# A fused recurrence and feed-forward kernel on one core: another written-out order of the same steps

## Chip, core and metric

One core of a Trainium2 chip. The metric is the device time of one execution in microseconds; the kernel before took 248.06 us as the median of three runs (247.24 to 250.97).

## The reference

Inputs are r, k, v, w, a, b of shape (4, 8, 768, 40): batch, heads, time, head dimension. A state of 40 x 40 for each batch and head is carried over 768 time steps; its outputs are the rows of a feed-forward block with a squared ReLU.

```python
for t in range(S):
    y[:, :, t] = np.einsum('bhd,bhde->bhe', rt, state)
    Sa = np.einsum('bhde,bhe->bhd', state, at)
    state_decay = state * wt[:, :, None, :] - np.einsum('bhd,bhe->bhde', Sa, bt)
    state = state_decay + np.einsum('bhd,bhe->bhde', vt, kt)
...
x = attn_out.transpose(0, 2, 1, 3).reshape(B * S, H * D)      # 3072 x 320
h = x @ w_in                                                  # 320 x 2048
g = np.maximum(h, 0.0) ** 2
return g @ w_out                                              # 2048 x 320
```

## The kernel before

The 768 steps are cut into 12 chunks (c = 0 to 11) of 64 steps. Within a chunk the recurrence is done with matmuls: products of decays are cumulative sums of log w, a unit-triangular system is solved by one correction, and the state goes from chunk to chunk. The 256 output rows of a chunk (4 batches x 64 steps) then go through the feed-forward block.

The kernel is a list of named steps. A step is an instruction on VectorE, ScalarE or GpSimd, a set of matmuls on PE, or one or two DMA issues; the number behind its name is the chunk. Steps that the text speaks of:

- Loads on SP: `ldw`, `ldk`, `ldb`, `lda`, `ldv`, `ldr` bring one tensor of one chunk into `raw_w`, `raw_kb`, `raw_a`, `raw_v`, `raw_r` (two buffers each; k and b share one), two issues of 160 KB. `lwi 0 k. x.` brings a quarter of one half of w_in's first 256 rows into a `G` buffer, `lwl 0` the last 64 rows into the buffer `CX` of odd chunks, `lwo 0 x.` an eighth of w_out into an `osb` buffer. `st` stores an output.
- Casts to bf16: `castK`, `castB`, `castA`, `castR`, `castV`; `cwi` makes `WIN`, `cwl` makes `WLAST`, `cwo` makes `WOUT`. For chunks 3 and later k and b are not cast but multiplied (`mulKB`).
- Decays: `ln` (logarithm of w), `hi` and `lo` (its two bf16 parts), `ci` and `cf` (cumulative sums on PE), `ex`, `ei`, `exw`, `ef`, `eg` (their exponentials).
- Turns on PE with identities: `TA`, `TR`, `TK`, `BK`, `TV`, `TS`, `XT`; their results leave PSUM by `tA`, `tR` or `tRw`, `tK`, `bK`, `tV`, `tS`, `xt`.
- Solve and state: `EN` (masked by `mEN`), `AS`, `EV`, `NU` (with `u0` and `u1` behind them), `SC`, `S` (with `s`, the new state `STb`). Output: `CX` (masked by `mCX`), `RS`, `Y` (with `y`, `yd`).
- Feed-forward: `F` and `FL` (eight matmuls on `WIN`, four on `WLAST`, for each quarter u0 to u3), `f` (ReLU), `q` (square), `O` (matmuls on `WOUT`), `o`.

A step's dependences come from what it reads and writes, buffers included. All PSUM results share four buffers, and an entry of the order such as `PE2` names the buffer that the step takes. Some steps can run on several engines, and the order names the engine. So three things are set by hand, by the text `ORDER`: the sequence on each engine's queue, the engine, and the PSUM buffer. `Plan.issue` reads it from left to right and emits:

```python
for entry in text.replace("\n", " ").split(";"):
    where, name = entry.split(None, 1)
    ...
    eng = where.rstrip("0123456789")
    assert i not in done and done.issuperset(o.preds), name
    ...
    for h in o.alloc:
        self.slot_of[h] = int(where[len(eng):])
    if o.emit[0] == "pe":
        for f in o.emit[2]:
            f()
    else:
        o.emit[1][eng]()
```

Each engine does its queue in sequence, and an instruction that waits holds up what stands behind it. SP's queue holds all loads but half of the first; a load into a buffer in use waits for the step that empties it. Because helpers emit everything, L390 is the line of nearly all matmuls, L394 and L397 those of the turns, L371 and L373 those of VectorE copies, L376 of ScalarE copies, L380 of GpSimd casts.

Of the kernel before, what the change touches and what calls it, by code (L numbers as in the profile page):

```python
# [91 lines left out]
eg 1; DVE mEN 0 g0; ACT ef 1; SP ldb 2; DVE castB 1; PE2 EV 0; DVE bK 0; SP ldv 1; PE3 TK 1; ACT
u0 0; PE0 TA 1; DVE tK 1 g1; ACT ln 2; POOL castR 0; PE NU 0; PE1 TR 0; DVE tA 1 g0; ACT u1 0 g0;
POOL castK 2; DVE tK 1 g0; SP lda 2; ACT u1 0 g1; POOL hi 2; ACT tRw 0; PE2 S 0 g0; POOL lo 2; PE
S 0 g1; DVE tA 1 g1; SP lwi 0 k1 x1; PE3 TV 0; DVE s 0 q0; SP ldw 3; POOL castB 2; PE0 cf 2; DVE s
0 q1; ACT tV 0; PE1 EN 1 g0; POOL castV 1 g1; DVE mEN 1 g0; PE2 EN 1 g1; SP lwi 0 k1 x3; SP lwo 0
x0; POOL castA 2; ACT eg 2; PE3 AS 1; DVE mEN 1 g1; PE1 TK 2; SP ldr 1; ACT castV 1 g0; DVE tK 2
g0; PE2 BK 1; ACT ef 2; SP lwl 0; PE EV 1; DVE tK 2 g1; ACT bK 1; PE0 TS 0; SP lwi 0 k1 x0; DVE u0
1; SP lwi 0 k0 x3; PE2 CX 0 g1; ACT tS 0; PE1 TA 2; DVE mCX 0 g1; SP ldv 2; PE NU 1; PE0 ci 2; DVE
tA 2 g1; ACT u1 1 g0; DVE tA 2 g0; ACT u1 1 g1; PE2 EN 2 g1; POOL castR 1; SP lwi 0 k1 x2; DVE mEN  # L100
2 g1; ACT exw 2; PE1 SC 1; SP lwi 0 k0 x1; PE3 TR 1; ACT ln 3; SP lwi 0 k0 x0; PE S 1 g0; PE S 1
g1; ACT tRw 1; SP lwi 0 k0 x2; PE2 CX 0 g0; POOL cwl 0; DVE s 1 q1; PE0 TV 1; SP lda 3; ACT hi 3;
DVE s 1 q0; POOL cwo 0 x0; PE3 BK 2; ACT tV 1; DVE mCX 0 g0; POOL lo 3; PE1 EN 2 g0; SP ldk 3; DVE
# [6 lines left out]
q1; SP lda 4; ACT castR 2; DVE mCX 1 g0; PE0 F 0 u2; ACT f 0 u1; SP ldv 3; PE1 TA 3; DVE cwo 0 x1;  # L110
ACT q 0 u0; PE2 TR 2; DVE tA 3 g0; PE3 RS 1; DVE tA 3 g1; PE Y 1; ACT tRw 2; POOL mulKB 3 h0; PE
FL 0 u2; SP lwo 0 x2; DVE y 1; PE1 TV 2; ACT f 0 u2; DVE yd 1; DVE mulKB 3 h1; PE2 FL 0 u3; ACT tV
2; POOL q 0 u2; PE3 XT 1; PE0 TK 3; SP lwo 0 x3; DVE xt 1; SP ldw 4; PE F 0 u3; DVE tK 3; ACT q 0
u1; POOL castV 3 g0; PE1 CX 2 g1; PE3 FL 1 u1; ACT f 0 u3; DVE mCX 2 g1; PE0 EN 3 g0; POOL castV 3
g1; PE F 1 u1; ACT cwo 0 x2; DVE mEN 3 g0; SP ldr 3; PE2 F 1 u2; ACT f 1 u1; POOL cwo 0 x3; PE1 EN
# [6 lines left out]
ldw 5; PE0 SC 3; DVE tV 3; PE S 3 g0; ACT castA 4; PE S 3 g1; PE2 cf 4; DVE s 3 q1; PE1 XT 2; ACT
ef 4; PE O 0 u1; DVE mulKB 4 h0; ACT xt 2; SP ldr 4; DVE mulKB 4 h1; PE2 TR 3; ACT cwo 0 x6; PE O
0 u2; DVE s 3 q0; ACT tRw 3; SP ldv 4; DVE cwo 0 x7; PE1 TA 4; PE0 TK 4; DVE tA 4 g1; PE2 CX 3 g1;
ACT tK 4; PE O 0 u3; DVE tA 4 g0; SP lda 6; DVE mCX 3 g1; PE1 F 2 u0; ACT o 0; PE2 CX 3 g0; ACT ln
5; PE0 EN 4 g0; DVE mCX 3 g0; PE3 FL 2 u3; PE FL 2 u0; POOL hi 5; PE F 2 u3; SP ldw 6; ACT f 2 u0;
DVE mEN 4 g0; POOL lo 5; PE2 F 2 u2; ACT q 1 u2; PE1 EN 4 g1; SP ldb 5; ACT f 2 u3; POOL q 2 u0;
# [24 lines left out]
O 3 u1; ACT ef 7; SP ldk 8; ACT ex 7 h0 g0; PE NU 6; ACT castR 6; PE2 TA 7; DVE u1 6 g0; ACT q 4
u2; PE0 TK 7; SP ldv 8; PE O 3 u2; DVE u1 6 g1; ACT tK 7; DVE tA 7 g0; PE O 3 u3; DVE tA 7 g1; DVE
hi 8; PE3 TR 6; DVE o 3; PE2 SC 6; POOL lo 8; ACT tR 6 g0; PE S 6 g0; PE S 6 g1; ACT tR 6 g1; PE0
XT 5; SP lda 9; DVE s 6 q1; PE1 TV 6; ACT xt 5; POOL castV 7 g1; PE3 TS 5; DVE tV 6; PE0 F 5 u0;
ACT tS 5; SP ldr 7; DVE s 6 q0; PE FL 5 u0; POOL castV 8 g1; PE1 ci 8 h0; ACT f 5 u0; PE3 EN 7 g0;
SP lda 8; POOL castV 7 g0; PE2 FL 5 u1; DVE mEN 7 g0; PE F 5 u1; POOL q 4 u3; ACT ex 8 h0 g1; ACT
# [929 lines left out]
```

## Time and profile before

| | |
|---|---|
| median of three runs | 248.06 us (247.24, 248.06, 250.97) |
| the profiled execution's own time | 247.57 us |
| its span | 245.6 us |
| busy: PE, PE weight loads | 222.8 us (91%), 176.5 us (72%) |
| busy: VectorE, ScalarE, GpSimd | 187.3 (76%), 173.4 (71%), 121.8 us (50%) |
| mean granted TensorE clock | 0.975 |
| DMA | 33.54 MB in 102,248 packets, 89,014 of them under 512 B |

The span is what the trace covers; the profiled execution's own time is 1.97 us longer and is comparable with the runs. A busy share is an average over a start, in which loads land, and a long dense part, in which PE hardly stands still, so the stages have to be read apart. A matmul's listed duration overlaps with that of its neighbours; the distance from start to start says what it costs.

### The profile page before, as it was taken

Reading aid. Unit: us, or ns where it says so; the run is one execution under the profiler, and the core shown is the slowest. Engines: PE = TensorE matmul, PEld = TensorE weight load, DVE = VectorE, ACT = ScalarE, POOL = GpSimd, SP = SyncE. Lnnn points to the kernel's source line nnn. Section 1 sums busy time; section 2 is a strip of 40 time slices with the busy share of each in tenths; the row PEclk is TensorE's granted clock in tenths of the full one; section 3 lists DMA queues with packets and bytes.
Section 4 is the critical chain, followed back from the end, with each engine's and each line's share of the span. In section 5 each row is a group of like instructions: output and inputs, shape, how many; then the busy total and the mean of one; then the engine's idle time right before and its main releaser. Section 6 shows DMA issues by size and latency. Waiting matters only on the chain.

```text
span 245.6 us, 12235 instructions
## 1 busy us (share of the span) xinstructions
PE 222.8 (91%) x5584; PEld 176.5 (72%) x5584; DVE 187.3 (76%) x234; ACT 173.4 (71%) x223; POOL 121.8 (50%) x111
## 2 busy tenths in 40 slices
PE   0668848999999999999999999999999899999993
PEld 0457737778887878778777777776877678887872
DVE  8589964888859878879989778798799788876600
ACT  3496963789788997977989757876876455660931
POOL 8245307528490887561619695327467940330150
PEclk9979985999999999999999999999999999999998
DMA  6998999989899988996984477687364020000403
GB/s 156 222 183 190 195 252 167 200 199 225 199 173 175 179 186 151 181 170 161 154 197 105 112 175 155 106 165 138 84 131 91 3 56 5 3 5 0 109 0 106
DMA packets 102248, 33.54 MB, mean 137 GB/s; under 512 B 89014, under 2 KB 101814, under 8 KB 101942
## 3 DMA queue, kind: packets, MB, share of 16 engines
q1 hardware_dynamic: 101014, 32.45, 64.0%
q8 instruction: 43, 0.70, 1.2%
q10 hardware_dynamic: 1184, 0.33, 0.6%
q14 instruction: 7, 0.06, 0.1%
HBM read 28.84 MB, written 3.93 MB: 133 GB/s over the span
## 4 chain that ended last, share of the span: by engine, by line
PE 77%; DMA 6%; DVE 6%; SPq 5%; ACT 3%; issue 1%; POOL 1%; ACTq 0%; POOLq 0%; DVEq 0%
PE pb L390 65%; PE pb L394 7%; PE pb L397 5%; DMA raw_r<-in_r_dram 3%; DMA raw_w<-in_w_dram 2%; DVE EN L689 1%; SPq L413 1%; SPq L443 1%; DMA raw_kb<-in_k_dram 1%; SPq L421 1%; DVE G L934 1%; DVE KBT L512 1%; DVE G L930 1%; SPq L1011 1%; ACT VUT L376 1%
## 5 line engine op out<-in xcount | busy, mean ns | idle before, releaser
L936 POOL TENSOR_TENSOR G<-G 128x1024 bf16<-128x1024 bf16 x25 | 47.6, 1911 | 40.1 <-ACT G L928 20.2
L390 PE MATMUL pb<-WOUT,G 128*128 128x320 bf16 (+1 forms) x400 | 57.3, 294 | 0.5 <-DVE G L930 0.5
L928 ACT ACTIVATE G<-pb 128x1024 bf16<-128x1024 f32 x41 | 41.5, 1022 | 18.4 <-PE pb L390 17.9
L390 PE MATMUL pb<-XT,WIN 128*128 128x256 bf16 x384 | 47.8, 273 | 0.4 <-ACT Gin L574 0.4
L390 PEld LDWEIGHTS <-G 128*128 128x128 bf16 x400 | 36.4, 98 | 14.2 <-issue 1.5
L390 PEld LDWEIGHTS <-WIN 128*128 128x128 bf16 x384 | 35.0, 98 | 7.7 <-issue 2.9
L689 DVE TENSOR_TENSOR CX<-pb,MSKI 128x1024 bf16<-128x1024 f32 x24 | 29.2, 1218 | 4.7 <-PE pb L390 3.4
L689 DVE TENSOR_TENSOR EN<-pb,MSK 128x1024 bf16<-128x1024 f32 x24 | 29.0, 1219 | 4.6 <-PE pb L390 4.4
L384 POOL TENSOR_TENSOR KB<-raw_kb,iG 128x640 bf16<-128x640 f32 x12 | 18.7, 1569 | 18.3 <-ACT iG L568 13.2
L384 POOL TENSOR_TENSOR lo<-lnW,hi 128x640 bf16<-128x640 f32 x11 | 16.0, 1458 | 17.2 <-PE pb L394 6.6
L781 DVE TENSOR_TENSOR STb<-pb,GT 64x640 bf16<-64x640 f32 x22 | 18.1, 821 | 8.2 <-POOL WLAST L380 5.5
L658 DVE TENSOR_TENSOR AR<-pb,GT 128x512 bf16<-128x512 bf16 x24 | 15.8, 684 | 6.4 <-PE pb L394 3.5
L390 PE MATMUL pb<-XT,WLAST 64*128 64x256 bf16 x192 | 17.1, 271 | 0.0
L590 ACT ACTIVATE GT<-pb 128x1024 f32<-128x1024 f32 x12 | 12.3, 1022 | 6.6 <-PE pb L390 4.0
L574 ACT ACTIVATE Gin<-pb 64x320 f32<-64x320 f32 x36 | 15.0, 426 | 2.6 <-PE pb L390 2.2
L376 ACT ACTIVATE AR<-pb 128x512 bf16<-128x512 bf16 (+1 forms) x15 | 10.2, 710 | 9.1 <-PE pb L397 4.0
L859 DVE TENSOR_TENSOR Yb<-pb,Gin 128x640 bf16<-128x640 f32 (+1 forms) x24 | 12.4, 552 | 5.0 <-PE pb L390 4.9
L390 PEld LDWEIGHTS <-EN 64*64 64x64 bf16 x768 | 14.0, 109 | 2.8 <-issue 1.7
L390 PE MATMUL pb<-UTI,hi 64*128 64x64 bf16 x192 | 8.3, 199 | 6.8 <-ACT hi L376 6.8
L376 ACT ACTIVATE VU<-pb 64x640 bf16<-64x640 f32 x15 | 10.5, 698 | 4.9 <-PE pb L390 3.7
L568 ACT ACTIVATE iG<-pb 128x640 f32<-128x640 f32 x18 | 12.6, 698 | 1.3 <-PE pb L390 1.2
L938 ACT ACTIVATE G<-G 128x1024 bf16<-128x1024 bf16 x12 | 12.6, 1054 | 0.1
(113 smaller groups left out, 439.9 us busy)
## 6 DMA issues: line engine op xcount, KB each, us to landing
raw_kb<-in_b_dram SPq DMA_DIRECT2D x24, 160.0 KB, 4.2
raw_kb<-in_k_dram SPq DMA_DIRECT2D x24, 160.0 KB, 4.6
raw_a<-in_a_dram SPq DMA_DIRECT2D x24, 160.0 KB, 3.6
raw_v<-in_v_dram SPq DMA_DIRECT2D x24, 160.0 KB, 4.4
raw_w<-in_w_dram SPq DMA_DIRECT2D x23, 160.0 KB, 4.8
raw_r<-in_r_dram SPq DMA_DIRECT2D x22, 160.0 KB, 5.1
out_dram<-osb SPq DMA_DIRECT2D x22, 160.0 KB, 3.1
osb<-in_moe_w_out_dram SPq DMA_DIRECT2D x8, 320.0 KB, 4.9
```

The costliest lines, as they stand in the source:

```text
L376: alts.append(("ACT", c_act(n), lambda: nc.scalar.activation(out=o_(), in_=i_(), func=ACTF.Copy, scale=1.0 if scale is None else scale)))
L384: return [("POOL", 40 + 2.35 * n, lambda: nc.gpsimd.tensor_tensor(out=o_(), in0=a_(), in1=b_(), op=op)), ("DVE", c_dve(n), lambda: nc.vect ...
L390: return lambda: nc.tensor.matmul(out=o_(), lhsT=l_(), rhs=r_(), start=start, stop=stop, skip_group_check=True)
L394: return lambda: nc.tensor.transpose(out=o_(), in_=i_(), identity=IDb[rows(g), :])
L568: ew(f"ei {c} h{jh}", [("ACT", c_act(2 * n), lambda hb=hb, jh=jh: nc.scalar.activation(out=iG[0][:].rearrange("p (g j) e -> p g (j e)", g= ...
L574: nc.scalar.activation(out=Gin[c % NGI][rows(g), NP * jh:NP * jh + NP, :].rearrange("p j e -> p (j e)"), in_=slot(hb, FP32)[rows(g), g, 0: ...
L658: ew(f"tA {c} g{g}", [("DVE", c_dve(512), lambda g=g: nc.vector.tensor_tensor(out=steps(AR[q2][:, 0, g]), in0=turned(ha, g), in1=steps(GT[ ...
L689: evac(f"m{nm} {c} g{g}", lambda s, n: [("DVE", c_dve(n), lambda: nc.vector.tensor_tensor(out=dst[q2][:, g, s].rearrange("p q i t -> p (q ...
L781: ew(f"s {c} q{q}", [("DVE", c_dve(2 * n), lambda q=q: nc.vector.tensor_tensor(out=STb[q2][rows(q), :, q, 0:D], in0=slot(hs, FP32)[rows(q) ...
L928: ("ACT", c_act(1024), lambda gb=gb, hf=hf: nc.scalar.activation(out=gb, in_=slot(hf, FP32)[:], func=ACTF.Relu)),
L936: ("POOL", 1900, lambda gv=gv: nc.gpsimd.tensor_tensor(out=gv, in0=gv, in1=gv, op=ALU.mult)),
L938: ("ACT", c_act(1024), lambda gv=gv: nc.scalar.activation(out=gv, in_=gv, func=ACTF.Square))],
```

## The change

Only the text `ORDER` changes. The steps, buffers and matmuls are the same, and each engine gets its steps in another sequence; some steps go to another engine and many PSUM results to another of the four buffers. The new sequence was laid out by a planner that was given longer transfers and scattered landing times. Changes of the matmul array's shape between neighbouring steps on PE number 201 before and 198 now. VectorE has 207 steps where it had 214, ScalarE 232 where it had 224 (two DMA issues among them), GpSimd 93 where it had 94.

```diff
-ORDER = """SP ldw 0; SP ldb 0; SP ldk 0; SP lda 0; ACT ln 0; SP ldw 1; ACT hi 0; DVE castB 0; DVE lo 0; DVE
-castK 0; PE0 cf 0; SP ldk 1; POOL castA 0; PE1 ci 0; ACT ef 0; SP lda 1; PE2 TA 0; SP ldv 0; ACT
...
+ORDER = """SP ldw 0; SP ldk 0; SP ldb 0; SP ldw 1; ACT ln 0; DVE hi 0; DVE lo 0; SP lda 0; PE0 cf 0; POOL
+castB 0; SP ldk 1; POOL castK 0; ACT eg 0; PE1 TK 0; SP ldb 1; ACT ln 1; PE2 ci 0; DVE tK 0 g0;
...
```

SP's queue at the loads of chunk 2, before:

```order
11 L453 DMA raw_r_84<-in_r_dram 128x1x320 x2
12 L421 DMA raw_kb_80<-in_k_dram 128x1x320 x2
13 L421 DMA raw_kb_80<-in_b_dram 128x1x320 x2
14 L436 DMA raw_v_87<-in_v_dram 64x16x40 x2
15 L443 DMA raw_a_82<-in_a_dram 128x1x320 x2
16 L1011 DMA G_128<-in_moe_w_in_dram 32x2048
```

and now:

```order
11 L453 DMA raw_r_84<-in_r_dram 128x1x320 x2
12 L421 DMA raw_kb_80<-in_b_dram 128x1x320 x2
13 L443 DMA raw_a_82<-in_a_dram 128x1x320 x2
14 L436 DMA raw_v_87<-in_v_dram 64x16x40 x2
15 L1011 DMA G_128<-in_moe_w_in_dram 32x2048
16 L421 DMA raw_kb_80<-in_k_dram 128x1x320 x2
```

k of chunk 2 (`ldk 2`) moved from the first of these five loads to the last, behind b, a, chunk 1's v and a quarter of half of w_in.

SP's queue at the loads of w_in, before:

```order
20 L453 DMA raw_r_85<-in_r_dram 128x1x320 x2
21 L1003 DMA CX_119<-in_moe_w_in_dram 64x1024 x2
22 L1011 DMA G_128<-in_moe_w_in_dram 32x2048
23 L1011 DMA G_129<-in_moe_w_in_dram 32x2048
24 L436 DMA raw_v_86<-in_v_dram 64x16x40 x2
25 L1011 DMA G_128<-in_moe_w_in_dram 32x2048
26 L1011 DMA G_129<-in_moe_w_in_dram 32x2048 x3
```

and now:

```order
20 L453 DMA raw_r_85<-in_r_dram 128x1x320 x2
21 L1011 DMA G_129<-in_moe_w_in_dram 32x2048
22 L1011 DMA G_128<-in_moe_w_in_dram 32x2048
23 L1011 DMA G_129<-in_moe_w_in_dram 32x2048
24 L1011 DMA G_128<-in_moe_w_in_dram 32x2048
25 L1011 DMA G_129<-in_moe_w_in_dram 32x2048
26 L436 DMA raw_v_86<-in_v_dram 64x16x40 x2
27 L1003 DMA CX_119<-in_moe_w_in_dram 64x1024 x2
```

The quarters of w_in now come before chunk 2's v, and w_in's last 64 rows (`lwl 0`, written to `CX_119`) moved from right behind chunk 1's r to the end of this piece. The first w_out load, which stood before the piece, now stands behind it.

SP's queue in the dense part, before:

```order
69 L443 DMA raw_a_83<-in_a_dram 128x1x320 x2
70 L453 DMA raw_r_85<-in_r_dram 128x1x320 x2
71 L443 DMA raw_a_82<-in_a_dram 128x1x320 x2
72 L429 DMA raw_kb_80<-in_b_dram 64x16x40 x2
73 L453 DMA raw_r_84<-in_r_dram 128x1x320 x2
74 L443 DMA raw_a_82<-in_a_dram 128x1x320 x2
```

and now:

```order
72 L453 DMA raw_r_84<-in_r_dram 128x1x320 x2
73 L429 DMA raw_kb_80<-in_b_dram 64x16x40 x2
74 L453 DMA raw_r_85<-in_r_dram 128x1x320 x2
75 L443 DMA raw_a_83<-in_a_dram 128x1x320 x2
76 L976 DMA out_dram<-osb_131 64x2x320 x2
77 L436 DMA raw_v_86<-in_v_dram 64x16x40 x2
```

Row 72 now is `ldr 10`, which was the 95th step of this queue; it stands ahead of b of chunk 8, r of chunk 7, a of chunk 9 and v of chunk 8, and takes the buffer that `castR 8` empties.

More of the change, by code (lines that the diff above doesn't have):

```diff
@@ L92 @@
[L92 to L103, printed above, removed]
@@ L110 @@
[L110 to L115, printed above, removed]
@@ L122 @@
[L122 to L127, printed above, removed]
@@ L152 @@
[L152 to L157, printed above, removed]
```

220 lines of the change are left out of this document (125 added, 95 removed).

## The prediction, on record before the changed kernel ran

> **What bounds the kernel now.** I read the windows first, by stages that the timeline suggested; the columns are the stage, its length, the busy time of PE, PE's weight loads, VectorE, ScalarE and GpSimd with their instructions, the granted TensorE clock, the DMA engines' share and GB/s.
>
> ```profile
> 0.00:20.00 20.00, 9.66 (x233) 7.64 (x233) 14.68 (x31) 11.34 (x14) 9.66 (x21) 0.91 0.86 184
> 20.00:34.00 14.00, 11.48 (x361) 9.73 (x356) 13.41 (x15) 11.99 (x14) 5.65 (x7) 1.00 0.95 215
> 34.00:42.30 8.30, 4.31 (x74) 3.98 (x75) 2.76 (x4) 2.65 (x4) 3.81 (x4) 0.59 0.97 183
> 42.30:50.00 7.70, 7.17 (x187) 5.75 (x186) 6.41 (x9) 5.98 (x9) 4.64 (x5) 1.00 0.96 198
> 50.00:180.00 130.00, 129.85 (x3405) 101.85 (x3403) 106.98 (x130) 107.15 (x142) 73.44 (x59) 1.00 0.79 160
> 180.00:192.00 12.00, 10.81 (x303) 8.45 (x302) 11.88 (x11) 8.03 (x12) 9.41 (x8) 1.00 0.51 100
> 192.00:241.60 49.60, 49.52 (x1036) 39.12 (x1034) 31.17 (x38) 25.90 (x31) 15.14 (x10) 1.00 0.12 29
> ```
>
> There are two kernels here. From 50 us on, PE is idle for 0.15 us of 130, for 1.19 us between 180 and 192, and for 0.08 us after that. Before 50 us it is idle for 10.34 + 2.52 + 3.99 + 0.53 = 17.4 us, the DMA engines are at 0.86 to 0.97, and one stage has a clock of 0.59. The matmuls stay the same, so from 50 us on a new order can gain some 1.4 us at most, and it can lose more. The start is decided by landings. There I read the timeline, of GpSimd and then of PE (start, length, engine, line, tiles, and in brackets the idle time before and what ended it).
>
> ```profile
> 37.22 0.72 POOL L380 CAST tR<-raw_r 128x640 bf16<-128x640 f32 x1 [7.93 <-DMA raw_r<-in_r_dram]
> 39.07 1.04 POOL L380 CAST WLAST<-CX 128x1024 bf16<-128x1024 f32 x1 [1.14 <-DMA CX<-in_moe_w_in_dram]
> 42.31 0.71 POOL L380 CAST VU<-raw_v 64x640 bf16<-64x640 f32 x1
> 47.11 3.01 POOL L380 CAST WIN<-G 128x1024 bf16<-128x1024 f32 x3 [2.83 <-DMA G<-in_moe_w_in_dram]
> ...
> 37.99 1.03 PE L397 MATMUL pb<-IDQ,tR 128*128 128x128 bf16 x8 [4.02 <-POOL tR L380]
> 38.96 1.04 PE L390 MATMUL pb<-VU,KB 128*64 128x40 bf16 x32
> 40.48 1.89 PE L397 MATMUL pb<-IDQ,VU 128*128 128x128 bf16 x16
> 42.15 1.11 PE L397 MATMUL pb<-IDQ,KBT 128*128 128x128 bf16 x16
> 48.68 1.03 PE L390 MATMUL pb<-XT,WIN 128*128 128x256 bf16 x8 [0.43 <-ACT Gin L574]
> 49.65 0.39 PE L390 MATMUL pb<-XT,WLAST 64*128 64x256 bf16 x4
> 50.17 0.41 PE L390 MATMUL pb<-AR,VUT 64*128 64x64 bf16 x16
> ```
>
> The reader is to see PE waiting 4.02 us for r of chunk 1 (TR 1), then at the low clock: the state product S 1 takes 1.04 us, the turn TV 1 1.89. Full clock and dense work begin when w_in has landed and been cast (47.11). Last comes CX 1 g1, at 50.17, the mark against which I measure: what the new order does before its own CX 1 g1, sooner or later, is gained or lost at the end.
>
> **The change part by part.** Sizes are those of the DMA issues: 2 x 160 KB for one tensor of one chunk, and for the weights
>
> ```profile
> G<-in_moe_w_in_dram SPq DMA_DIRECT2D x8, 256.0 KB
> CX<-in_moe_w_in_dram SPq DMA_DIRECT2D x2, 256.0 KB
> ```
>
> A load with more bytes ahead of it in SP's queue is taken to land later by these bytes over the stage's GB/s. These are estimates, since single landings scatter.
>
> First matmuls. The new order takes hi 0 from ScalarE to VectorE and puts the two casts of k and b on GpSimd, so lo 0 need not stand behind a cast.
>
> ```profile
> 6.01 0.74 ACT L376 ACTIVATE hi<-lnW 128x640 bf16<-128x640 f32 x1
> ...
> 6.94 0.49 DVE L371 CAST tKB<-raw_kb 128x640 bf16<-128x640 f32 x1
> 7.34 0.82 DVE L386 TENSOR_TENSOR lo<-lnW,hi 128x640 bf16<-128x640 f32 x1
> ```
>
> 6.01 + 0.49 + 0.82 = 7.32 instead of 8.16: 0.84 us sooner. EV 0 however needs v of chunk 0, which is the eighth load in both queues. I count nothing and keep -0.84 for the range.
>
> Chunk 2's k. ldk 2 now stands behind ldb 2, lda 2, ldv 1 and one quarter of w_in: 1,216 KB more, at 215 GB/s 5.7 us.
>
> ```profile
> 18.77 2.78 DMA raw_kb<-in_k_dram
> ...
> 26.38 0.48 PE L390 MATMUL pb<-STb,AR 128*64 128x80 bf16 x16 [0.59 <-ACT VUT L376]
> 26.79 0.64 PE L394 MATMUL pb<-IDb,tKB 64*128 64x64 bf16 x32
> ...
> 28.91 0.68 PE L390 MATMUL pb<-VU,EN 64*64 64x40 bf16 x32
> ...
> 30.15 6.95 DMA raw_r<-in_r_dram
> ...
> raw_r<-in_r_dram SPq DMA_DIRECT2D x22, 160.0 KB, 5.1
> ```
>
> The chain of waits has it landing at 21.55, hence 27.2 now, or 29.1 if it scatters as r did (6.95 against a median of 5.1). castK 2 is on ScalarE, and behind it in that queue stand eg 2, ef 2, bK 1, ln 3, tS 0 and both u1 1; on PE, TK 2 and behind it AS 1, EV 1 (28.91 before), TS 0, NU 1. With a cast (0.72) and then TK and AS (0.64 and 0.48), EV 1 comes at 29.0 to 30.9: 0 to 2 us late. That is work before the next wait, and r absorbs it.
>
> Chunk 1's r is the twentieth load in both, 64 KB sooner now, so TR 1 again comes near 38. But NU 1, CX 0 g0, TA 2, SC 1, both S 1 and Y 0 now stand between the late EV 1 and TR 1. PE's 4.02 us fall into pieces below 2 us, so I expect the full clock. The same shapes at full clock, before:
>
> ```profile
> 21.52 0.62 PE L397 MATMUL pb<-IDQ,tR 128*128 128x128 bf16 x8 [0.29 <-POOL tR L380]
> 22.73 0.69 PE L390 MATMUL pb<-VU,KB 128*64 128x40 bf16 x32 [0.59 <-ACT VU L376]
> 23.34 1.07 PE L397 MATMUL pb<-IDQ,VU 128*128 128x128 bf16 x16
> ```
>
> The three save 0.41 + 0.35 + 0.82 = 1.6 us. After TR 1 come two EN (0.41 each) and TV 1, so BK 2 starts at 37.95 + 0.62 + 0.82 + 1.07 = 40.4 instead of 42.15.
>
> This lead meets the weights. The eight quarters of w_in now end 1,152 KB sooner (6 us, near 41), but lwl, its last 64 rows, stands behind 1,536 KB more: at 190 GB/s 8.1 us, so its cast starts at 39.07 + 8.1 = 47.2 and ends at 48.2. FL 0 u0 needs it and stands on PE ahead of NU 2 and CX 1 g1. EV 2 waits for v of chunk 2 (192 KB more: 42.31 + 1.0 = 43.3, then two casts of 0.71, so 44.8), F 0 u0 ends at 46.5, and PE waits 1.7 us. FL 0 u0 (0.39) and NU 2 (0.68) put CX 1 g1 at 49.25: 0.9 us sooner. TS 1, done by 50.17 before, now comes later, which takes back 1.05:
>
> ```profile
> 44.33 1.05 PE L397 MATMUL pb<-IDQ,STb 128*128 128x128 bf16 x16
> ```
>
> The start comes out at **+0.1 us**. Bounds: without a wait for lwl, CX 1 g1 comes 1.7 us sooner; with r's scatter on lwl, 1.9 later.
>
> Behind the mark. VectorE gets mCX 2 g1, mCX 2 g0, mEN 3 g0, mEN 3 g1 in a row, and FL 1 u3 waits for the last one's PSUM buffer.
>
> ```profile
> L689 DVE TENSOR_TENSOR CX<-pb,MSKI 128x1024 bf16<-128x1024 f32 x24 | 29.2, 1218 | 4.7 <-PE pb L390 3.4
> ```
>
> The EN masks have the same shape; four times 1.22 is 4.9 us; PE has between them CX 2 g0, two F (0.97 each from start to start), two FL, two EN, RS, Y and AS, some 4.2. I take **+0.7**, bounds 0 and 1.5.
>
> The rest. The other groups change places and engines but not in number; changes of the array's shape fall from 201 to 198, not worth a term. Engine totals move little: eight more instructions on ScalarE, seven fewer on VectorE, one fewer on GpSimd; from 50 to 180 us ScalarE is busy 107 of 130 and VectorE as much. The 1.19 us between 180 and 192 come from a square and an STb on VectorE that this order also has; I keep them, bound -1.2.
>
> ```profile
> 184.49 2.85 DVE L934 TENSOR_TENSOR G<-G 128x1024 bf16<-128x1024 bf16 x1
> 191.23 0.64 PE L394 MATMUL pb<-IDb,VU 64*128 64x64 bf16 x32 [0.65 <-DVE STb L781]
> ```
>
> The sum is 0.1 + 0.7 = 0.8 us on the profiled execution's 247.57, so 248.4. That execution lies 0.49 us below the median of the runs, so the forecast is **248.9 us**.
>
> **The rivals.** One: the gap at TR 1 is simply filled. If k and lwl come no later than they are needed, the 4.02 us and the 1.6 us of low clock are a gain that nothing takes back: 248.06 - 5.6 = 242.4. For it: both stand in the trace. Against it: DMA at 0.95 and more, so what lands sooner makes something else land later.
>
> Two, slower: the load queue stalls in the dense part. ldr 10, 95th in SP's queue before, is 72nd now, ahead of ldb 8, ldr 7, lda 9 and ldv 8. It needs the buffer that castR 8 empties, and castR 8 now stands near 130 on ScalarE.
>
> ```profile
> L453 SPq DMA_DIRECT2D raw_r<-in_r_dram x22: 563/598/3194, 15.2 to 181.2; - x22
> ...
> DMA to landing us min/median/max: 4.8/5.1/5.3
> 138.91 1.87 POOL L384 TENSOR_TENSOR KB<-raw_kb,iG 128x640 bf16<-128x640 f32 x1 [1.95 <-ACT iG L568]
> 141.25 0.72 ACT L376 ACTIVATE tR<-raw_r 128x640 bf16<-128x640 f32 x1
> ```
>
> At 0.6 us an issue ldr 7 is out at 134 and lands at 139, against casts due between 139 and 141. If ldr 10's two issues take the longest 3.19 instead, 5.2 more, castR 7 runs some 4 late; behind it on ScalarE stand ex 8, u1 and f results, whose PSUM buffers PE needs. A microsecond late costs one: 248.9 + 4.3 = 253.2, and 258 if ldr 7 does the same. It decides from a landing past 141. For it: several other loads changed places as well (lda 4 by 2.5 MB), and this part has nothing to gain. Against it: DMA share 0.79 there.
>
> Three: the low clock comes back at TK 2 or FL 0 u0. If PE stands still there for about 4 us, as it did before TR 1, the next 8 us run at 0.59 and three groups lose 1.6 us: 250.5. [...]
>
> **How the numbers follow.** 0.37 for the forecast, 0.06 for the third rival, 0.40 for the second, 0.17 for the first. Within 2% (243.1 to 253.0, about what a measurement of this kernel can tell from no change) lie the forecast and the third: 0.43. Faster 0.17, slower 0.40. The forecast's own range takes the bounds 1.7 + 0.7 + 0.8 + 1.2 below and 1.9 + 0.8 above: 244.5 to 251.6. The full range reaches into both rivals: 243.0 to 256.0.
>
> **What would show it.** Right: castK 2 on ScalarE waits for raw_kb past 27; no stage before 50 us at a clock of 0.59; PE stands before the matmuls with WLAST, near 47, for 1 to 3 us; from 52 us on PE busy all but 1 to 2 us. Wrong: a gap at TR 1 as long as before; WLAST cast before 45; PE idle for several us between 130 and 150 behind ScalarE's tR<-raw_r, or elsewhere behind a load; an end more than 5 us from 245.6.

## The result and the profile after

The new order took 246.72 us (median of 6 runs, 244.25 to 248.11) beside 248.76 us of the old one. The ratio is **0.990, with an interval of 0.986 to 0.994**. Timed again with twelve runs (e13 below) it was 0.9906 (0.987 to 0.994). The new order is 1% faster; the forecast was 0.3% slower. Executions over 1.5% longer than the fastest of their kernel are left out of the ratios (not of the medians), and the profiled executions of e14 and e16 were such. The profiled execution took 245.21 us, with a span of 242.8 us where the old one had 245.6.

The windows after, by the same stages and with the same columns as before:

```profile
0.00:20.00 20.00, 9.94 (x208) 7.60 (x209) 14.77 (x31) 10.19 (x14) 10.11 (x22) 1.00 0.87 181
20.00:34.00 14.00, 10.57 (x320) 9.13 (x319) 11.40 (x12) 12.16 (x15) 4.32 (x6) 0.91 0.97 220
34.00:42.30 8.30, 7.40 (x205) 6.32 (x203) 7.21 (x10) 5.42 (x5) 4.72 (x6) 0.95 0.97 192
42.30:50.00 7.70, 6.47 (x171) 4.62 (x172) 5.37 (x8) 5.59 (x11) 2.47 (x4) 1.00 1.00 234
50.00:180.00 130.00, 129.54 (x3371) 101.13 (x3364) 106.09 (x127) 105.33 (x141) 84.16 (x67) 1.00 0.79 158
180.00:192.00 12.00, 11.90 (x327) 9.60 (x326) 8.58 (x10) 10.79 (x17) 8.95 (x7) 1.00 0.50 91
```

Read the first number behind the length, PE's busy time. From 34 to 42.3 us PE is busy for 7.40 us where it was 4.31: the gap before TR 1 is gone. In the four stages before 50 us together, though, PE is idle for 15.6 us where it was 17.4: of the 3.1 us, 1.3 come back in the stages beside it. From 50 to 180 us it is idle for 0.46 us where it was 0.15, so the dense part lost next to nothing. From 180 to 192 us it is idle for 0.10 us where it was 1.19. The clock column has no 0.59 any more, but it has 0.91 and 0.95.

The start, from the timeline of PE and then of GpSimd:

```profile
30.37 0.64 PE L394 MATMUL pb<-IDb,tKB 64*128 64x64 bf16 x32 [1.46 <-ACT tKB L376]
31.35 1.04 PE L390 MATMUL pb<-VU,EN 64*64 64x40 bf16 x32
32.33 1.89 PE L397 MATMUL pb<-IDQ,STb 128*128 128x128 bf16 x16
37.60 0.62 PE L397 MATMUL pb<-IDQ,tR 128*128 128x128 bf16 x8
40.71 1.05 PE L397 MATMUL pb<-IDQ,KBT 128*128 128x128 bf16 x16 [0.32 <-DVE EN L689]
46.45 0.39 PE L390 MATMUL pb<-XT,WLAST 64*128 64x256 bf16 x4 [0.41 <-POOL WLAST L380]
47.39 0.41 PE L390 MATMUL pb<-AR,VUT 64*128 64x64 bf16 x16
```

```profile
36.11 0.72 POOL L380 CAST tR<-raw_r 128x640 bf16<-128x640 f32 x1
40.32 2.03 POOL L380 CAST WIN<-G 128x1024 bf16<-128x1024 f32 x2 [3.50 <-DMA G<-in_moe_w_in_dram]
42.29 1.50 POOL L380 CAST VU<-raw_v 64x640 bf16<-64x640 f32 x2
45.36 1.04 POOL L380 CAST WLAST<-CX 128x1024 bf16<-128x1024 f32 x1 [1.57 <-DMA CX<-in_moe_w_in_dram]
```

TK 2 waits 1.46 us for the late k of chunk 2, and EV 1 (1.04 instead of 0.68) and TS 0 (1.89 instead of 1.07) then run at the low clock. TR 1 no longer waits for r. The cast of WLAST starts at 45.36 us, and PE waits 0.41 us for it. CX 1 g1 runs at 47.39 us where it was 50.17; but TS 1, done before that mark in the old order, now comes behind it, so less than these 2.8 us is won.

The place at 184 us, which the forecast left as it was. First the old order's PE row, then the GpSimd rows beside its 2.85 us square on VectorE, then the new order's VectorE:

```profile
188.53 1.25 PE L390 MATMUL pb<-WOUT,G 128*128 128x320 bf16 x8 [0.54 <-DVE G L930]
```

```profile
183.56 0.72 POOL L380 CAST tA<-raw_a 128x640 bf16<-128x640 f32 x1
184.22 0.71 POOL L380 CAST VU<-raw_v 64x640 bf16<-64x640 f32 x1
184.90 1.89 POOL L936 TENSOR_TENSOR G<-G 128x1024 bf16<-128x1024 bf16 x1
```

```profile
184.73 1.23 DVE L930 TENSOR_SCALAR G<-pb 128x1024 bf16<-128x1024 f32 x1 [0.76 <-PE pb L390]
185.87 0.68 DVE L934 TENSOR_TENSOR G<-G 128x1024 bf16<-128x1024 bf16 x1
```

and the new order's GpSimd:

```profile
186.03 2.27 POOL L936 TENSOR_TENSOR G<-G 128x1024 bf16<-128x1024 bf16 x1 [1.98 <-DVE G L930]
```

The old order's square q 7 u0 on VectorE started at 184.49 us and ended at 187.34, 0.55 us after GpSimd's square (184.90 + 1.89 = 186.79). In the new order GpSimd is idle for the 1.98 us before 186.03, so it is idle when VectorE's square of that stretch (here q 8 u3) starts, and this square takes 0.68 us; GpSimd's own square, which starts beside it, takes 2.27 instead of 1.89. That pointed to a cause which the forecast did not have.

### The profile page after: what moved, and what is told of

Same layout as the page of the kernel before. It is cut to its first block, busy times and chain, and to the rows that moved or that the text cites. A ratio compares the mean times of both kernels' runs of the same rounds, so it can differ in the third digit from the quotient of the medians.

```text
span 242.8 us, 12250 instructions
## 1 busy us (share of the span) xinstructions
PE 223.2 (92%) x5584; PEld 175.7 (72%) x5584; DVE 182.8 (75%) x227; ACT 178.8 (74%) x231; POOL 119.9 (49%) x110
## 4 chain that ended last, share of the span: by engine, by line
PE 77%; SPq 9%; DMA 5%; ACT 2%; issue 2%; POOL 2%; DVE 1%; POOLq 0%; ACTq 0%
PE pb L390 66%; PE pb L394 7%; PE pb L397 4%; SPq L1003 2%; SPq L1011 2%; DMA raw_w<-in_w_dram 2%; DMA CX<-in_moe_w_in_dram 2%; SPq L453 2%; SPq L413 1%; SPq L421 1%; DMA raw_r<-in_r_dram 1%; DVE EN L689 1%; SPq L436 1%; POOL lo L384 1%; DVE CX L689 1%
## 5 line engine op out<-in xcount | busy, mean ns | idle before, releaser
L936 POOL TENSOR_TENSOR G<-G 128x1024 bf16<-128x1024 bf16 x24 | 45.7, 1909 | 32.2 <-ACT G L928 29.9
L928 ACT ACTIVATE G<-pb 128x1024 bf16<-128x1024 f32 x39 | 39.5, 1022 | 15.4 <-PE pb L390 15.3
L390 PE MATMUL pb<-XT,WIN 128*128 128x256 bf16 x384 | 48.4, 273 | 0.0
L384 POOL TENSOR_TENSOR KB<-raw_kb,iG 128x640 bf16<-128x640 f32 x13 | 21.3, 1641 | 9.0 <-DMA raw_kb<-in_b_dram 8.3
L384 POOL TENSOR_TENSOR lo<-lnW,hi 128x640 bf16<-128x640 f32 x9 | 13.2, 1466 | 11.4 <-ACT hi L376 11.0
L390 PEld LDWEIGHTS <-EN 64*64 64x64 bf16 x768 | 14.8, 112 | 2.7 <-issue 1.6
L376 ACT ACTIVATE AR<-pb 128x512 bf16<-128x512 bf16 (+1 forms) x17 | 11.4, 694 | 6.7 <-PE pb L394 2.9
L938 ACT ACTIVATE G<-G 128x1024 bf16<-128x1024 bf16 x15 | 15.5, 1052 | 0.0
L930 DVE TENSOR_SCALAR G<-pb 128x1024 bf16<-128x1024 f32 x9 | 11.0, 1220 | 5.3 <-PE pb L390 5.3
L380 POOL CAST hi<-lnW 128x640 bf16<-128x640 f32 x7 | 5.0, 719 | 18.2 <-ACT lnW L532 9.5
```

The lines of the kernel that those rows point to most:

```text
L384: return [("POOL", 40 + 2.35 * n, lambda: nc.gpsimd.tensor_tensor(out=o_(), in0=a_(), in1=b_(), op=op)), ("DVE", c_dve(n), lambda: nc.vect ...
L390: return lambda: nc.tensor.matmul(out=o_(), lhsT=l_(), rhs=r_(), start=start, stop=stop, skip_group_check=True)
L928: ("ACT", c_act(1024), lambda gb=gb, hf=hf: nc.scalar.activation(out=gb, in_=slot(hf, FP32)[:], func=ACTF.Relu)),
L936: ("POOL", 1900, lambda gv=gv: nc.gpsimd.tensor_tensor(out=gv, in0=gv, in1=gv, op=ALU.mult)),
L938: ("ACT", c_act(1024), lambda gv=gv: nc.scalar.activation(out=gv, in_=gv, func=ACTF.Square))],
```

## Experiments

The theory to begin with: two gains, one at the start and one at 184 us, where in the old order VectorE's square took 2.85 us beside GpSimd's instructions, against 0.68 in the new order with GpSimd idle (the text calls this a clash). The rivals: all of it at the start, or all of it in the dense part. The edits are to `ORDER` alone; a ratio is to the old order on the same chip, and a "PE idle" figure is the length of a window less PE's busy time.

### e1, e2: halves joined at F 0 u3

```diff
 e1: the new order to F 0 u3, then the old order's remaining steps in their sequence
 e2: the old order to F 0 u3, then the new order's remaining steps in their sequence
```

> The new order up to the step F 0 u3 (about 55 us), then the old order. Theory (two gains: the start, and a square on VectorE at 184 us that no longer stands behind GpSimd): the start's 1.3 us are kept (CX 1 g1 near 47.4), the 1.2 us are not: PE idle 1.0 to 1.4 us between 178 and 192, the bf16 square on VectorE there again 2 to 3 us long; ratio to before 0.995 (0.992 to 0.998). Rival A, all of the gain is the start's: 0.990 to 0.991. Rival B, all of it lies in the dense part: 0.999 to 1.002.

> The old order up to the step F 0 u3, then the new order. Theory: CX 1 g1 near 50.2 as before, r of chunk 1 with its gap of 4 us; PE idle under 0.3 us between 178 and 192; ratio 0.995 (0.992 to 0.998). Rival A (all from the start): 1.000. Rival B (all from the dense part): 0.990.

e1 was 1.0119 (1.006 to 1.018), e2 0.9951 (0.992 to 0.999). The windows just behind the joint, of e1 and then of e2:

```profile
50.00:60.00 10.00, 8.06 (x194) 6.81 (x192) 7.26 (x12) 9.43 (x10) 4.82 (x4) 1.00 0.77 170
...
178.00:194.00 16.00, 14.81 (x394) 11.62 (x391) 15.55 (x16) 11.64 (x16) 10.96 (x9) 1.00 0.41 86
```

```profile
50.00:60.00 10.00, 7.78 (x200) 6.33 (x196) 8.61 (x10) 7.58 (x8) 3.39 (x2) 1.00 0.76 164
...
178.00:194.00 16.00, 15.91 (x380) 12.89 (x374) 12.87 (x14) 14.71 (x21) 10.69 (x8) 1.00 0.57 106
```

Both lose about 2 us from 50 to 60 us. At F 0 u3 the old order has issued sixteen steps (TR 2, TK 3, XT 1 and both mulKB 3 among them) that the new one has not, so the joint makes a sequence that neither order has. In e2 part of the loss is a clash made there: a mulKB on VectorE takes 2.50 us beside GpSimd's square, and PE waits 1.29 us for it. So the two ratios say nothing about the start, and that e2 met the expected 0.995 is luck. What they do say: the idle time at 184 us (16.00 - 14.81 = 1.19 us) goes with the old dense part, not with one execution.

### e3: the two squares apart

```diff
 GpSimd in the old order, around 185 us
-castV 11 g1; q 7 u3; q 7 u1; castR 11
+castV 11 g1; q 7 u1; q 7 u3; castR 11
```

> The old order with one step of GpSimd moved: the square q 7 u3 stands behind q 7 u1 instead of ahead of it, so GpSimd is idle when VectorE comes to its own square q 7 u0. Theory (VectorE's bf16 square cannot run beside a GpSimd instruction and waits for it to end): q 7 u0 takes 0.7 to 1.2 us instead of 2.85, F 8 u0 and O 7 u0 come earlier, PE's idle between 180 and 192 falls from 1.2 to 0.2 us or less, ratio 0.996 (0.994 to 0.998). Rival (the 2.85 us were a disturbance of that one execution): the old kernel's other executions do not have it, so nothing is gained: 1.000. Rival 2 (the late square comes back as a late O 7 u3): 1.000 with the idle moved to 192 to 200.

0.9967 (0.994 to 0.999); median 247.19 beside 248.65 us. VectorE around the place, and the window:

```profile
184.88 0.98 DVE L942 TENSOR_TENSOR G<-G 128x1024 bf16<-128x1024 bf16 x1
186.06 2.43 DVE L938 TENSOR_SCALAR G<-pb 128x1024 bf16<-128x1024 f32 x2 [0.19 <-PE pb L398]
```

```profile
178.00:194.00 16.00, 16.00 (x431) 12.35 (x429) 14.03 (x16) 11.72 (x16) 11.25 (x9) 1.00 0.41 86
```

Two neighbouring squares of GpSimd, changed about, make VectorE's square 0.98 instead of 2.85 us long (it ends at 185.86, 0.54 us behind a cast of GpSimd that ends at 185.32) and take PE's idle time from 1.19 to 0.00 us. The theory's numbers came (0.7 to 1.2 us for the square, 0.2 us or less of idle time); neither rival's did.

### e4: the gap before TR 1 filled, alone

```diff
 PE in the old order
-SC 1; TR 1; S 1 g0; S 1 g1; CX 0 g0; TV 1
+SC 1; S 1 g0; S 1 g1; CX 0 g0; TR 1; TV 1
```

> The old order with one turn moved: TR 1 stands behind both S 1 and CX 0 g0 on PE, and its copy tRw 1 behind it, so that chunk 1's r is waited for with less work left. Theory (the start ends on the landings of w_in and on EV 2, not on r): the gap before TR 1 falls from 4.0 to 2.0 to 3.0 us, BK 2 comes 1 to 2 us sooner, but EV 2, F 0 u0 and CX 1 g1 stay within 0.4 us of 46 to 47 and 50.2: ratio 0.999 to 1.001. Rival (the gap is the loss, as my first rival had it): CX 1 g1 1 to 2 us sooner, 0.992 to 0.996.

0.9992 (0.996 to 1.002): nothing. PE in the stretch:

```profile
38.25 0.62 PE L405 MATMUL pb<-IDQ,tR 128*128 128x128 bf16 x8
39.98 1.05 PE L405 MATMUL pb<-IDQ,KBT 128*128 128x128 bf16 x16 [0.22 <-ACT AR L384]
47.80 1.05 PE L398 MATMUL pb<-XT,WIN 128*128 128x256 bf16 x8 [1.49 <-POOL WIN L388]
49.00 0.40 PE L398 MATMUL pb<-AR,VUT 64*128 64x64 bf16 x16
```

The gap is gone (TR 1 follows at once), and BK 2 comes 2.2 us sooner than the profile of before had it. But F 0 u0 waits 1.49 us for the cast of w_in, and CX 1 g1 comes at 49.00, only 0.3 to 0.6 us ahead of the 49.27 to 49.64 that the old start gave in e2, e3 and e6 (the expectation had it near 50.2, which only the profile of before shows). The longest wait in the profile of before was not what ended the start.

### e5, e6, e9: halves joined at S 3 g1

At S 3 g1 (some 74 us) the two orders have done the same steps but for the squares q 1 u0 and q 1 u1 (and the cast castA 4 and the load ldw 5, which stand right beside the joint in both).

```diff
 e5: the new order to S 3 g1, then the old one
 e6: the old order to S 3 g1, then the new one
 e9: e5 with the two squares set apart
-POOL castA 4; DVE q 1 u1; POOL q 1 u0; DVE s 3 q1
+POOL castA 4; DVE s 3 q1; ... DVE tA 4 g0; POOL q 1 u1; ... DVE mCX 3 g0; DVE q 1 u0
```

> The new order up to S 3 g1 (about 74 us), where both orders have done the same steps but for two squares, then the old order. Theory (the start gives 0.5 to 1.0 us, the clash of the two squares at 184 us 1.2): CX 1 g1 near 47.4, PE busy from 52 to 75 us but for 0.5 us, the long square and 1.0 to 1.4 us of PE idle again between 178 and 194; ratio 0.9965 (0.994 to 0.999). Rival A (all of the gain from the start): 0.991. Rival B (all from the dense part): 1.000.

> The old order up to S 3 g1, then the new order. Theory: the start as before (gap at TR 1 of 2 to 4 us, CX 1 g1 at 49.3 to 50.2), no square over 1 us on VectorE and PE idle under 0.3 us between 178 and 192; ratio 0.9945 (0.992 to 0.997). Rival A: 1.000. Rival B: 0.991. My forecast's slower rival (loads such as ldr 10 stall the dense part): 1.01 and more; it would show here alone.

> The kernel of e5_new_to_75 with the two squares at the joint set apart as the new order has them: q 1 u1 on GpSimd behind tA 4 g0, q 1 u0 on VectorE behind mCX 3 g0. In e5 the square q 1 u1 took 1.67 us on VectorE beside GpSimd's q 1 u0, and PE then waited 1.68 us for VectorE. Theory (the same clash as at 184 us): that wait goes, the one at 184 us stays; ratio to before 0.9965 (0.993 to 0.999). Rival (the joint was short of a landing): PE's wait between 74 and 80 us stays above 1 us; 1.002.

e5 was 1.0021 (0.998 to 1.006), outside what the theory gave. The joint had made a second clash by accident, as VectorE and GpSimd show:

```profile
72.56 1.67 DVE L943 TENSOR_TENSOR G<-G 128x1024 bf16<-128x1024 bf16 x1
74.27 0.83 DVE L790 TENSOR_TENSOR STb<-pb,GT 64x640 bf16<-64x640 f32 x1
```

```profile
71.80 1.89 POOL L945 TENSOR_TENSOR G<-G 128x1024 bf16<-128x1024 bf16 x1
```

71.80 + 1.89 = 73.69, and VectorE's square ends 0.55 us later, at 74.24; everything behind it on VectorE is late, and PE waits:

```profile
77.59 0.41 PE L403 MATMUL pb<-IDb,tA 64*128 64x64 bf16 x16 [1.68 <-DVE STb L790]
```

In e9 the two squares are apart and that wait is gone (PE is busy for 9.91 of the 10 us from 70 to 80, in e5 for 8.32); the clash at 184 us is still there, 14.81 of 16. Its ratio is 0.9991 (0.996 to 1.002), just above what the theory gave (0.994 to 0.999). So the new order's start, taken alone, is worth 0.2 us by the times, with an uncertainty of 0.8. e6, the old start with the new order from 75 us on, was 0.9935 (0.990 to 0.998). By these two, most of the gain lies behind 75 us.

### e10: new start, and both pairs of squares apart

```diff
 e9 and e3 together
```

> The new order up to S 3 g1, then the old one with both pairs of squares apart: e9_joint_mended and e3_square_apart together. Theory (the new order's gain is its start and the absence of the clash, and nothing else): the same time as the new order, 0.990 (0.987 to 0.994); PE idle under 0.3 us between 178 and 194. Rival (the rest of the new order is worth something by itself): 0.994 and more.

0.9935 (0.991 to 0.997), median 246.63 us beside e9's 248.20 on the same chip. The one moved square is worth 1.5 us in e3 and 1.6 here by the medians, 0.8 and 1.4 by the ratios. The window from 178 to 194 us:

```profile
178.00:194.00 16.00, 16.00 (x430) 12.36 (x428) 14.03 (x16) 11.65 (x16) 11.33 (x9) 1.00 0.41 86
```

The expected 0.990 lies just outside the interval, and the new order itself was 0.9906. Whether the remaining 0.003 is real, the intervals (0.987 to 0.994 and 0.991 to 0.997) do not tell; e6 against e3 leaves the same 0.003, with intervals as wide.

### e7, e11: k of chunk 2 early

```diff
 SP in the new order (e7), and in e10 (e11)
-ldr 0; ldb 2; lda 2; ldv 1; lwi 0 k1 x2; ldk 2
+ldr 0; ldk 2; ldb 2; lda 2; ldv 1; lwi 0 k1 x2
```

> The new order with the load ldk 2 put back where the old one has it, behind r of chunk 0 and ahead of b, a and v. Theory (the start ends on v of chunk 2, w_in and its last rows, so the late k of chunk 2 costs nothing at the end): TK 2 at 27 to 28.5 without its 1.46 us of waiting, EV 1 at 28.5 to 30, no or a shorter stretch at the low clock between 31 and 35, TR 1 at 36.5 to 37.6, but F 0 u0 and CX 1 g1 within 0.5 us of 45.0 and 47.4: ratio 0.990 (0.987 to 0.993), as the new order. Rival (what the late k shows, 1.5 us of waiting and 1.4 us of low clock, is lost at the end): 0.979 to 0.983.

> e10_start_and_apart with ldk 2 early as in e7_k_early: the three things that the runs point to, together. Theory: k's place gives nothing at the end, so 0.990 as e10. Rival (without the low clock at EV 1 the start is sometimes sooner): 0.985 to 0.988, faster than both kernels.

e7 was 0.9905 (0.988 to 0.993), the same as the new order. PE in e7, and one of its windows:

```profile
29.47 0.64 PE L403 MATMUL pb<-IDb,tKB 64*128 64x64 bf16 x32
30.68 0.68 PE L399 MATMUL pb<-VU,EN 64*64 64x40 bf16 x32
37.62 0.68 PE L406 MATMUL pb<-IDQ,tR 128*128 128x128 bf16 x8 [1.10 <-POOL tR L389]
46.12 0.68 PE L399 MATMUL pb<-VU,EN 64*64 64x40 bf16 x32 [2.02 <-POOL VU L389]
```

```profile
38.05:41.47 3.42, 3.27 (x56) 3.05 (x54) 2.56 (x4) 1.18 (x2) 0.47 (x1) 0.50 1.13 180
```

TK 2 does not wait and EV 1 runs at full clock, so the 1.46 us of waiting and these 1.4 us of low clock are gone; then PE waits 1.10 us for r and 2.02 us for v, and the clock is 0.50 from 38.05 to 41.47 us instead. F 0 u0 comes at 46.73 and CX 1 g1 at 48.65 us, 1.7 and 1.3 us later than the expected 45.0 and 47.4. The late k cost nothing at the end because PE waited for the next landings instead, at the low clock again. e11 was 0.9956 (0.993 to 0.998), not the 0.990 expected: no gain over e10 either.

### e8, e12, e16: what ends the start

```diff
 SP in the new order
 e8:  -ldv 2; lwl 0; ldk 3; lwo 0 x0; lwo 0 x1; ldr 2
      +ldv 2; ldk 3; lwo 0 x0; lwo 0 x1; ldr 2; lwl 0
 e12: -ldr 1; five quarters of w_in; ldv 2; lwl 0
      +ldr 1; lwl 0; five quarters of w_in; ldv 2
 e16: -ldw 3; seven quarters of w_in with ldr 1 among them; ldv 2; lwl 0
      +the same loads; lwl 0; ldw 3   (and chunk 3's decays later on all engines)
```

> The new order with lwl (w_in's last 64 rows) four loads later: behind k of chunk 3, two w_out pieces and r of chunk 2, 1,280 KB more ahead of it. This prices the term that my forecast mis-sized. By my forecast's price (190 GB/s) its cast starts 6.9 us later, at 52.2; by the rate that the new order shows from 42.3 to 50 us (234 GB/s) 5.6 later, at 51.0. Theory: PE stands for it one for one before FL 0 u0, 5 to 7 us, and the low clock follows: ratio 1.012 to 1.02. Rival (work behind FL 0 u0 was short of other landings anyway, so the wait is partly free): PE's wait of 5 us, but the end only 2 us later: 0.998.

> The new order with lwl (512 KB) behind r of chunk 1, as the old order has it; six quarters of w_in and v of chunk 2 get 512 KB more ahead of them. Theory (w_in's eight quarters and v bind as soon as lwl does not): WLAST cast at 38 to 39.5, PE no longer waits before FL 0 u0, but the casts of w_in and v come 2 to 2.5 us later, so EV 2 near 46 and F 0 u0 near 47: ratio to before 0.993 to 1.000, slower than the new order. Rival (lwl alone binds): 0.988 to 0.990.

> The new order with w of chunk 3 (ldw 3, 320 KB) loaded behind lwl instead of ahead of most of w_in, and with what it feeds (ln 3, hi 3, lo 3, ci 3, ei 3, ex 3, cf 3, ef 3) moved some 8 us back on all engines, behind u1 2 g1 on ScalarE and FL 0 u2 on PE; f 0 u2 goes to VectorE. Theory (the start ends when the bytes up to lwl have come, whatever their order): 320 KB less at 200 to 234 GB/s, so lwl's cast starts 1.4 to 1.6 us sooner, near 43.9, FL 0 u0 near 45.0 instead of 46.5. If the moved work of chunk 3 costs nothing, ratio to before 0.984 to 0.987; if TA 3 and mulKB 3 then come late, PE stands 1 to 2 us between 54 and 60 and the ratio is that of the new order, 0.990. Rival (landings scatter more than 320 KB count): lwl's cast at 45 or later, 0.990 or more.

(The quarters of w_in that lwl passes in e12 are five, not six.)

e8: 1.022 (1.016 to 1.028). e12: 1.000 (0.997 to 1.003). e16: 1.0091 (1.005 to 1.013). The casts on GpSimd, in that order, and PE's wait in e8:

```profile
52.51 1.04 POOL L389 CAST WLAST<-CX 128x1024 bf16<-128x1024 f32 x1 [7.87 <-DMA CX<-in_moe_w_in_dram]
```

```profile
46.37 1.49 POOL L389 CAST VU<-raw_v 64x640 bf16<-64x640 f32 x2 [0.75 <-DMA raw_v<-in_v_dram]
```

```profile
44.11 1.04 POOL L389 CAST WLAST<-CX 128x1024 bf16<-128x1024 f32 x1 [2.05 <-DMA CX<-in_moe_w_in_dram]
```

```profile
53.60 0.61 PE L399 MATMUL pb<-XT,WLAST 64*128 64x256 bf16 x4 [6.05 <-POOL WLAST L389]
```

With 1,280 KB more ahead of it (e8) lwl's cast starts 7.1 us later than the new order's 45.36, 180 GB/s; PE stands 6.05 us for it, and the median is 7.6 us above that of e7 beside it (254.17 and 246.62), so this load does bind. With lwl early (e12) v of chunk 2 is the late one (46.37 instead of 42.29), and the gain of the new order is gone; the clock from 30 to 54 us is 0.72 here and 0.93 in the new order, so how much of the loss is v's own stays open. With 320 KB less ahead of it (e16) lwl's cast starts at 44.11, 1.25 us sooner, and 0.7 sooner than the earliest of nine other profiles with the same bytes ahead of it (44.77 to 46.40): the bytes ahead count, as expected, though by how much one execution cannot tell. The time did not follow. In the profile F 0 u0 itself ran later than in the new order (47.31) and PE is idle for 2.8 of the 16 us from 46 to 62; whether that is the cause in the other executions is not shown.

### e13, e14, e15: the new order again, with a clash, with v sooner

```diff
 e14: GpSimd (and ScalarE, from which two casts come) in the new order
-q 8 u2; q 7 u1; castA 11; castV 10 g0
+q 8 u2; castA 11; castV 10 g0; castV 10 g1; castR 10; q 7 u1
 e15: SP and GpSimd in the new order
-lwi 0 k1 x0; lwi 0 k0 x0; lwi 0 k1 x3; lwi 0 k0 x1; ldv 2   cwi 0 k1h0; cwi 0 k0h0; castV 2
+ldv 2; lwi 0 k1 x0; lwi 0 k0 x0; lwi 0 k1 x3; lwi 0 k0 x1   castV 2; cwi 0 k1h0; cwi 0 k0h0
      PE: NU 2 ahead of FL 0 u0; VectorE: u1 2 g0 ahead of f 0 u0
```

> The new order itself, unchanged, timed beside the next two. Theory: 0.990 to 0.993, so that the start (0.9991 in e9_joint_mended) and the clash (0.9967 in e3_square_apart) leave 0.5 to 1 us to the rest of the order. Rival (start and clash are all): 0.994 to 0.996.

> The new order with a clash put in: on GpSimd the casts castA 11, castV 10 g0, castV 10 g1 and castR 10 (the last two from ScalarE) stand ahead of the square q 7 u1, so GpSimd is busy from 184.1 to 186.9 us, when VectorE comes to its square q 8 u3 at 185.9. Theory: q 8 u3 takes 1.5 to 2.2 us instead of 0.68, tV 9 and f 8 u1 behind it come about 1 us later, PE stands 0.6 to 1.3 us between 184 and 194, and the ratio is 0.004 above that of the new order beside it. Rival (the casts have one input and do not hold VectorE up, or the delay is absorbed): square at 0.7 to 0.9, PE idle under 0.2, same time as the new order.

> The new order with v of chunk 2 loaded four quarters of w_in sooner (ahead of lwi 0 k1 x0), its two casts ahead of those of w_in on GpSimd, NU 2 ahead of FL 0 u0 on PE and u1 2 g0 ahead of f 0 u0 on VectorE. Theory (v, and behind it lwl, end the start): castV 2 done by 41 us, EV 2 at 42 to 43.5 instead of 44.4, F 0 u0 near 44, FL 0 u0 still behind lwl's cast at 46.4, with NU 2 ahead of it: 0.5 to 1.2 us sooner, ratio to before 0.986 to 0.989, faster than both orders. Rival (w_in's quarters, now 320 KB later, bind instead): F 0 u0 at 45 or later and the same ratio as the new order.

e13: 0.9906, as the theory had it. e14: 0.993 (0.988 to 0.998), not to be told from e13, and its clash hardly came about: in the profiled execution VectorE's square (q 8 u3) took 0.99 us, and it was GpSimd's next cast that took longer, 1.22 us:

```profile
190.56 1.22 POOL L389 CAST tR<-raw_r 128x640 bf16<-128x640 f32 x1
```

That cast takes 0.72 us elsewhere. So e14 did not test what it was made for. e15: 0.9936 (0.990 to 0.997), no gain. EV 2 came sooner, as expected, but then the quarters of w_in, 320 KB later, bind, much as its rival had it (F 0 u0 at 44.74, not 45 or later):

```profile
42.62 0.68 PE L399 MATMUL pb<-VU,EN 64*64 64x40 bf16 x32
44.74 1.05 PE L399 MATMUL pb<-XT,WIN 128*128 128x256 bf16 x8 [1.44 <-POOL WIN L389]
46.62 0.39 PE L399 MATMUL pb<-XT,WLAST 64*128 64x256 bf16 x4 [0.22 <-POOL WLAST L389]
```

Behind the start this execution also has a clash of its own: a mulKB on VectorE takes 2.40 us instead of 0.81 beside GpSimd's square (75.54 to 77.43 us), and PE waits 1.29 us for it. GpSimd's square had itself waited behind a cast of w_out for a landing.

```profile
75.72 2.40 DVE L395 TENSOR_TENSOR KB<-raw_kb,iG 128x640 bf16<-128x640 f32 x1
78.17 0.52 PE L403 MATMUL pb<-IDb,KB 64*128 64x64 bf16 x24 [1.29 <-DVE KB L395]
```

None of the variants beats the new order.

## Why the prediction was wrong

**The rest (kept at 0, bound -1.2).** This is the step that failed most. I took the 1.19 us between 180 and 192 us as a property of the steps, "a square and an STb on VectorE that this order also has". The row that I quoted had the answer in it: 2.85 us for an instruction that takes 0.68 elsewhere. It was GpSimd's instructions beside it (the square that the new order has in this stretch is another one, and stands elsewhere), and what stands beside what is exactly what an order changes. e3 and e10 price it at 0.8 to 1.6 us; by PE's idle time in the trace it is 1.2. In the traces the longer one of the two ends behind the other: VectorE's squares end 0.55 us behind GpSimd's instruction in the old order and in e5, and in e14 GpSimd's cast took 1.22 us, where it takes 0.72 elsewhere. Which of the two comes first they do not show so simply: in the old order VectorE's square is recorded from 184.49 us, while a cast of GpSimd ran that ended at 184.93; GpSimd's square began only at 184.90 and took its 1.89 us, and VectorE's ended behind it, at 187.34.

**Behind the mark (+0.7).** Four masks in a row are there (60.07 to 64.70 us), but PE waits 0.20 us for the last of them and is idle for only 0.46 us from 50 to 180 us where it was 0.15. By this profile the term is 0.3 at most. I had set the masks' time against the PE steps that stand between them; what else PE had to run meanwhile I left out, and no run tested it.

**Start (+0.1).** The pieces: *First matmuls*, counted 0, right: hi 0 did not start before 6.95 us on VectorE. *Chunk 2's k*: its cast started at 29.58 us, past the 27.2 to 29.1 forecast, and EV 1 at 31.35 instead of 29.0 to 30.9; that this is absorbed was right (e7), and the clock falls with it (0.50 from 31.36 to 34.77 us), which the forecast did not have. *Gap at TR 1*: it did go, and BK 2 came at 40.71 against the forecast 40.4; the clock was low ahead of it and full at it (TR 1 takes 0.62 us, BK 2 1.05). That pieces below 2 us, or a wait of 1.7 us, keep the full clock was my estimate, and no run shows such a bound: in the new order a clock of 0.50 followed a longest wait of 1.46 us, and in e7 the matmuls behind a wait of 2.02 us ran at the full clock (EV 2 0.68 us). *Weights*: lwl's cast starts at 45.36 us, not 47.2, and PE waits 0.41 us, not 1.7. I had moved lwl by 1,536 KB from its own old place, where the profiled execution had it at 39.07; the old start had it at 37.95 to 38.49 in e2, e3, e4 and e6, so the anchor was late by 0.6 to 1.1 us, and the 8.1 us for the way were too long as well (6.9 to 7.4 by these). A nearer anchor stood in the same trace: by the sizes, the last quarter of w_in had 8,640 KB up to its end in the old queue and was cast at 47.11; lwl now has 8,320. 320 KB at the stage's 198 GB/s are 1.6 us: 45.5. (Ten profiles with these bytes ahead of lwl, the new order's among them, have it at 44.77 to 46.40.) What the start then gave is 0.2 us with an uncertainty of 0.8 by the times (e9), where the pair of profiles shows more, since the profiled execution of before had a late start (CX 1 g1 at 50.17, with the same start at 49.27, 49.32 and 49.64 in e2, e3 and e6).

**The rivals.** The first, 242.4 us, had the gap as the loss; e4 took the gap away alone and gained nothing. The second, slower at 253.2 with a chance of 0.40, did not come: with PE idle for 0.46 us in 130, no load stalls the dense part of the profiled execution, ldr 10 or another. The third, the low clock at TK 2, did come, after a wait of 1.46 us and not of 4, and cost nothing that e7 could give back.

**The account.** The result of 246.7 us lies inside the forecast's own range, 244.5 to 251.6. That is luck: the forecast had the change going the other way, and no mechanism stood behind the bound that came, the -1.2. Forecast (1.003 of the old order's median) and result (0.990) lie 1.3% apart, 3.3 us: the clash is 0.8 to 1.6 of it, the masks 0.4, the start 0.3 by e9. What is left, 1 to 2 us, the runs do not settle, and its cause stays open: it may be the new order behind 75 us apart from the clash (e10 against e13), or the width of the intervals, each of which is some 0.8 us to either side.

## What to carry to other kernels

When a row shows one instance of an instruction far longer than its group's others, look at what the other engines do beside it: such a wait belongs to the order, and any new order may remove or create it (e3 removed one by changing two neighbours about, e5 made one). Price a moved load from the load that stood at about the same number of bytes in the old queue, not from its own old place, and from more than one execution (one load here, lwl, speaks for it). The longest wait in a start that is bound by landings need not be the loss: when it was filled (e4), or when another was taken away (e7), PE waited for the next landing.
